# A decode-attention kernel moved from a tile framework to hand-placed buffers, semaphores and short loops

## Chip, cores and metric

One core of one Trainium2 chip; the other cores are idle. The metric is the device time of one execution in microseconds (us), a median over several runs.

Engine names: PE is TensorE (PEld its weight loads), DVE is VectorE, ACT is ScalarE, POOL is GpSimd, SP is SyncE. SP computes nothing here; it issues the loads. They are carried by 16 DMA engines.

## The reference

The function adds three terms for a batch of 8 tokens, one token each. Only the attention term is large: it reads 32 heads x 4096 keys and values of 128 numbers for each of the 8 batch entries, in bf16.

```python
xn = layernorm(A_x)                                   # (8, 1, 576)
q  = (xn @ wq) as (8, 32, 1, 128)
p  = softmax(q . k_cache * 128**-0.5)                 # k_cache (8, 32, 4096, 128)
o  = p . v_cache                                      # v_cache (8, 32, 4096, 128)
attention = o as (8, 1, 4096) @ wo                    # wo (4096, 576)
mlp = gelu(layernorm(xn) @ w1 + b1) @ w2 + b2         # w1 (576, 4608), w2 (4608, 576)
return A_x + attention + mlp
```

K and V are 2 x 268 MB; all weights together are 20 MB. There are two floating-point operations for every number read, and the profile below has the load queue at 99.5%, DVE at 65% and PE at 59%: the kernel is about moving bytes.

## The kernel before

The work is cut into 32 tiles of 8 heads. A tile's K (and its V) is 128 partitions x 64 KB = 8.4 MB. They lie in a ring of five chunks of 32 KB a partition; K and V of successive tiles take two chunks each in turn. Every fifth pair wraps around the end of the ring and is then loaded as two halves.

```python
    def chunks(t, kind):
        return [(3 + 2 * (2 * t + kind) + h) % NCH * CHUNK for h in range(2)]

    def load_kv(cache, t, at):
        src = cache_v[cache.tensor.name][bass.ds(t * P, P), :]
        if at[1] > at[0]:
            nc.sync.dma_start(out=ring[:, at[0]:at[0] + 2 * CHUNK], in_=src)
        else:
            for h in range(2):
                nc.sync.dma_start(
                    out=ring[:, at[h]:at[h] + CHUNK], in_=src[:, h * CHUNK:(h + 1) * CHUNK])
```

A tile is worked off in eight blocks: DVE multiplies a block of K with the query (`prod`), PE adds groups of the products with an identity matrix (`s_ps`), DVE reduces what is left (`sc`). ACT takes the exponential, DVE spreads it over heads (`ebd`), PE multiplies it with V (`o_ps`), and some small operations divide by the sum and store the result in `Ox`.

```python
        for x in range(2 * NCB):                       # scores of one tile
            ...                                        # DVE: prod = K block * query
            for d in range(nd):                        # PE: s_ps += identity @ part of prod
                nc.tensor.matmul(ps, lhsT=ident, rhs=prod[...], start=..., stop=...)
            if x > 0:
                reduce(x - 1)                          # DVE: sc; ACT: exp after every half
            ...
```

The main loop takes five tiles a turn, so that the ring's addresses repeat; its last turn leaves by another arm, which loads the output weights and finishes. The framework finds the waits, allots the semaphores and writes the loop's branches for all five engines.

```python
    with tc.For_i(0, LAST + NCH, NCH, iteration_sync="reg_based") as it:
        attend(it, 0)
        load_tile(it + 1, 1)
        attend(it + 1, 1)
        with tc.If(it < LAST, preferred_fallthrough_block=False) as turn:
            ...                                        # tiles 2, 3, 4 of the turn
        with turn.Else():
            project()                                  # w2, wo, last matmuls, output
```

`project()` ends with the cast of the two output halves, one on DVE and one on ACT, and their stores:

```python
        fin = const.tile([P, ND], BF16, name="fin")
        nc.vector.tensor_copy(out=fin[:B], in_=acc[0][:B])
        nc.sync.dma_start(out=out2[:, :ND], in_=fin[:B])
        nc.scalar.activation(out=fin[OP:OP + B], in_=acc[1][OP:OP + B], func=ACT.Copy)
        nc.scalar.dma_start(out=out2[:, ND:], in_=fin[OP:OP + B])
```

The softmax here doesn't subtract the row's maximum and nothing guards it: scores larger than these inputs give would overflow.

## Time and profile before

| | before |
|---|---|
| time, median | 1298.54 us (1298.42 to 1298.85, 12 runs) |
| span in the profile, first to last instruction | 1297.0 us |
| load queue: share of 16 engines, bytes, rate | 99.5%, 556.94 MB, 430 GB/s |
| busy: DVE, PE | 838.2 us (65%), 768.3 us (59%) |

These lines are from the page of the kernel before. The first gives busy time (share of the span) and instructions of each engine; "DMA" is the mean busy share, in tenths, of the 16 DMA engines in 40 equal slices of the span; "GB/s" is what they moved in each. The "q" lines are DMA queues: packets, MB, and the time of their packets as a share of 16 engines' span. q1 carries the loads, q8 and q14 carry instructions.

```profile
PE 768.3 (59%) x4780; PEld 327.0 (25%) x4780; DVE 838.2 (65%) x733; ACT 52.8 (4%) x173; POOL 1.4 (0%) x11
...
DMA  9999999999999999999999999999999999999997
GB/s 407 445 416 435 440 424 446 424 426 445 431 426 437 437 427 436 441 418 445 437 420 443 431 428 445 422 430 442 435 427 434 439 424 443 437 419 440 437 426 321
...
q1 hardware_dynamic: 12832, 556.94, 99.5%
q8 instruction: 8, 0.13, 0.0%
```

No compute engine is near its limit; the load queue is, in every slice but the last. Two more things can be read from the trace's own record of each packet (one packet is one row of a load, one partition's contiguous bytes). A row of 64 KB takes 2422 ns on its engine, a row of 32 KB 1217 ns. And from the first load packet's start (1.785 us) to the last one's end (1290.559 us) pass 1288.8 us, while all packets' time divided by 16 is 1289.0 us: the engines have no room left.

What the loads wait for, and what waits for them, is in the timeline. These are the last tile but one and the last tile of the kernel before (start, duration, engine, line, operation; in brackets the idle time before and what ended it):

```profile
1209.87 4.49 DVE L342 TENSOR_TENSOR prod<-ring,qb 128x4096 bf16<-128x4096 bf16 x2 [11.10 <-DMA ring<-in_A_k_cache_dram]
...
1222.07 0.33 SPq L142 DMA_DIRECT2D ring<-in_A_k_cache_dram  x1
...
1241.54 0.21 DVE L377 RECIPROCAL rec<-tot 128x8 f32<-128x8 f32 x1 [2.54 <-PE tot L374]
1248.44 4.50 DVE L342 TENSOR_TENSOR prod<-ring,qb 128x4096 bf16<-128x4096 bf16 x2 [4.84 <-DMA ring<-in_A_k_cache_dram]
...
1279.38 0.21 DVE L377 RECIPROCAL rec<-tot 128x8 f32<-128x8 f32 x1 [2.54 <-PE tot L374]
```

A tile's arithmetic takes some 31 us from the first product (1248.44) to the reciprocal of the sum (1279.38), when V is used up. Tiles follow each other at 38.8 us on average (that is 128 x 2 rows x 2422 ns over 16 engines). DVE waits for K between them.

The groups of instructions (busy us, mean ns of one, then idle time before them and what ended it):

```profile
L348 PE MATMUL s_ps<-prod,ident 128*128 128x512 bf16 x2048 | 564.9, 430 | 463.3 <-DVE prod L342 463.1
L342 DVE TENSOR_TENSOR prod<-ring,qb 128x4096 bf16<-128x4096 bf16 x256 | 581.9, 2284 | 176.9 <-DMA ring<-in_A_k_cache_dram 176.7
L334 DVE TENSOR_REDUCE sc<-s_ps 128x32 f32<-128x512 f32 x256 | 175.6, 686 | 98.0 <-PE s_ps L348 50.1
```

A warning about one view. The chain of waits of this kernel (work followed back from the last instruction, shares of the span) reads:

```profile
issue 40%; DMA 23%; DVE 15%; PEld 11%; PE 9%; ACT 2%; DVEq 0%; PEldq 0%; SPq 0%; ACTq 0%
```

It follows one release at a time, and goes through DVE and PE although the queue was full throughout. The packet records and the DMA row decide, not this.

### The profile page before, as it was taken

The numbers are of one execution on the slowest core, as the hardware profiler recorded it, in microseconds if no ns is written. First come the engines' busy times: TensorE is split into PE (matmuls) and PEld (weight loads), VectorE is DVE, ScalarE is ACT, GpSimd is POOL, SyncE is SP. The second block draws the span as 40 slices with busy tenths as digits, with TensorE's granted clock in tenths as the row PEclk, the third lists the DMA queues.
The fourth block names the chain that finished last, engine by engine and source line by source line (L and its number), as shares of the span: only waits on it lengthen the run. The fifth ranks groups of instructions, "written<-read, shape, count | busy, mean of one in ns | idle before, by whom it ended". The sixth has DMA issues, their size and how long they took to land.

```text
span 1297.0 us, 12687 instructions
## 1 busy us (share of the span) xinstructions
PE 768.3 (59%) x4780; PEld 327.0 (25%) x4780; DVE 838.2 (65%) x733; ACT 52.8 (4%) x173; POOL 1.4 (0%) x11
## 2 busy tenths in 40 slices
PE   5555667455666465576455566455567455567466
PEld 1122222122222222222122222122223122222123
DVE  4656677566677565677555677565677666677663
ACT  1100000000000000000000000000000000000000
POOL 0000000000000000000000000000000000000000
PEclk9788888788988778988777998787898788898779
DMA  9999999999999999999999999999999999999997
GB/s 407 445 416 435 440 424 446 424 426 445 431 426 437 437 427 436 441 418 445 437 420 443 431 428 445 422 430 442 435 427 434 439 424 443 437 419 440 437 426 321
DMA packets 12882, 557.12 MB, mean 430 GB/s; under 512 B 1452, under 2 KB 1477, under 8 KB 1735
## 3 DMA queue, kind: packets, MB, share of 16 engines
q1 hardware_dynamic: 12832, 556.94, 99.5%
q8 instruction: 8, 0.13, 0.0%
q10 hardware_dynamic: 38, 0.02, 0.0%
q14 instruction: 4, 0.02, 0.0%
HBM read 556.94 MB, written 0.01 MB: 429 GB/s over the span
## 4 chain that ended last, share of the span: by engine, by line
issue 40%; DMA 23%; DVE 15%; PEld 11%; PE 9%; ACT 2%; DVEq 0%; PEldq 0%; SPq 0%; ACTq 0%
DMA ring<-in_A_k_cache_dram 20%; PEld L348 9%; DVE prod L342 9%; PE s_ps L348 4%; PE o_ps L367 4%; DVE sc L334 3%; DVE ebd L320 3%; DMA ring<-in_A_wo_dram 2%; PEld oT L380 1%; ACT ob L371 1%; PE tot L374 1%; ACT e L314 1%; PE oT L380 1%; DMA ring<-in_A_wq_dram 0%; PEld L367 0%
## 5 line engine op out<-in xcount | busy, mean ns | idle before, releaser
L348 PE MATMUL s_ps<-prod,ident 128*128 128x512 bf16 x2048 | 564.9, 430 | 463.3 <-DVE prod L342 463.1
L342 DVE TENSOR_TENSOR prod<-ring,qb 128x4096 bf16<-128x4096 bf16 x256 | 581.9, 2284 | 176.9 <-DMA ring<-in_A_k_cache_dram 176.7
L348 PEld LDWEIGHTS <-ident 128*128 128x128 bf16 x2048 | 222.1, 108 | 798.0 <-issue 634.5
L334 DVE TENSOR_REDUCE sc<-s_ps 128x32 f32<-128x512 f32 x256 | 175.6, 686 | 98.0 <-PE s_ps L348 50.1
L367 PE MATMUL o_ps<-ring,ebd 128*32 128x512 bf16 x2048 | 122.2, 380 | 22.0 <-DVE ebd L320 22.0
L320 DVE TENSOR_TENSOR ebd<-e,head 128x1024 bf16<-128x1024 bf16 x64 | 78.1, 1221 | 16.5 <-ACT e L314 16.5
L367 PEld LDWEIGHTS <-ebd 128*32 128x32 bf16 x2048 | 48.6, 96 | 93.3 <-DVE ebd L320 37.8
L314 ACT ACTIVATE e<-sc 128x128 bf16<-128x128 f32 x64 | 19.8, 310 | 1077.6 <-DVE sc L334 1077.6
L377 DVE RECIPROCAL rec<-tot 128x8 f32<-128x8 f32 x32 | 6.6, 208 | 81.4 <-PE tot L374 81.4
L380 PE MATMUL oT<-selc,ob 128*128 128x8 f32 x256 | 33.7, 258 | 18.1 <-ACT ob L371 18.1
L380 PEld LDWEIGHTS oT<-selc,ob 128*128 128x128 f32 x256 | 31.0, 191 | 20.8 <-ACT ob L371 15.9
L382 DVE TENSOR_TENSOR on<-oT,rec 128x8 bf16<-128x8 f32 x32 | 5.3, 166 | 45.1 <-PE oT L380 43.7
L371 ACT ACTIVATE ob<-o_ps 128x512 f32<-128x512 f32 x32 | 19.1, 597 | 117.1 <-PE tot L374 117.1
L374 PEld LDWEIGHTS tot<-headf,Ep 128*128 128x128 f32 x128 | 16.6, 188 | 13.6 <-issue 13.6
L374 PE MATMUL tot<-headf,Ep 128*128 128x8 f32 x128 | 19.6, 261 | 0.0
L275 PE MATMUL h_ps<-ring,prod 128*32 128x384 bf16 x54 | 12.5, 863 | 0.0
L314 ACT ACTIVATION_READ_ACCUMULATOR e<-sc 128x1 f32 x64 | 12.0, 187 | 0.0
L286 DVE TENSOR_SCALAR prod<-prod 96x384 f32<-96x384 f32 x2 | 0.7, 352 | 13.0 <-ACT prod L285 13.0
L193 PE MATMUL tp<-ident,ring 8*128 8x8 bf16 x18 | 1.4, 198 | 12.3 <-DVE ring L189 12.3
L383 DVE TENSOR_TENSOR Ox<-on,quad 128x32 bf16 x32 | 6.2, 193 | 1.1
L308 PE MATMUL acc<-ring,OT 128*8 128x288 bf16 x64 | 4.6, 286 | 1.3 <-DMA ring<-in_A_wo_dram 1.3
L438 DVE CAST fin<-acc 8x288 bf16<-8x288 f32 x1 | 0.4, 445 | 7.3 <-PE acc L308 7.3
(67 smaller groups left out, 55.6 us busy)
## 6 DMA issues: line engine op xcount, KB each, us to landing
ring<-in_A_v_cache_dram SPq DMA_DIRECT2D x14, 4096.0 KB
ring<-in_A_k_cache_dram SPq DMA_DIRECT2D x12, 4096.0 KB, 31.7
ring<-in_B_w_dram SPq DMA_DIRECT2D x3, 1728.0 KB, 18.0
ring<-in_B_w_dram SPq DMA_DIRECT2D x2, 2592.0 KB, 30.1
ring<-in_A_wq_dram SPq DMA_DIRECT2D x3, 1536.0 KB, 9.4
ring<-in_A_wo_dram SPq DMA_DIRECT2D x1, 2016.0 KB, 24.7
ring<-in_A_wo_dram SPq DMA_DIRECT2D x1, 1440.0 KB, 25.4
ring<-in_A_wo_dram SPq DMA_DIRECT2D x1, 720.0 KB, 24.3
```

The lines of the kernel that those rows point to most:

```text
L275: nc.tensor.matmul(hps[j][s * MP:(s + 1) * MP], lhsT=lhsT, rhs=wv[:, r0:r0 + HK, :], **flags)
L314: nc.scalar.activation(out=e, in_=sc, func=ACT.Exp, scale=scale, accum_out=Ep[:, h:h + 1])
L320: nc.vector.tensor_tensor(out=ebd, in0=e[:].rearrange("p (j c) -> p j c", c=4).unsqueeze(2).to_broadcast([P, J, G, 4]), in1=head[:, :].uns ...
L334: nc.vector.tensor_reduce(out=scs[h][:, n * CB:(n + 1) * CB], in_=banks[x], axis=AX.X, op=ALU.add)
L342: nc.vector.tensor_tensor(out=prod, in0=k[h][:, n * CB:(n + 1) * CB, :], in1=qb[:, bass.ds(t, 1), :].to_broadcast([P, CB, Dh]), op=ALU.mult)
L348: nc.tensor.matmul(ps, lhsT=ident, rhs=prod[:, :, d * DL:(d + 1) * DL], start=(d == 0), stop=(d == nd - 1))
L367: nc.tensor.matmul(ps[m * MP:(m + 1) * MP, :], lhsT=ebds[h][:, j], rhs=v[h][:, 4 * j:4 * j + 4, :], start=(h == 0 and j < M), stop=(h == 1 ...
L371: nc.scalar.activation(out=ob[:].rearrange("r c d -> r (c d)"), in_=ps, func=ACT.Copy)
L374: nc.tensor.matmul(tot, lhsT=Ep[:, h:h + 1].to_broadcast([P, P]), rhs=headf, start=(h == 0), stop=(h == 1))
L377: nc.vector.reciprocal(out=rec, in_=tot)
L380: nc.tensor.matmul(oT, lhsT=ob[:, c, :], rhs=selc[:, c, :], start=(c == 0), stop=(c == 3))
L383: nc.vector.tensor_tensor(out=Ox[:, bass.ds(t, 1)].rearrange("p o g m -> p (o g) m"), in0=on[:, :].unsqueeze(2).to_broadcast([P, G, M]), i ...
```

## The change

The intent: give up the framework and its loop machinery, and place everything by hand. The arithmetic and the loaded bytes stay. What differs:

- K has two homes that overlap in one chunk, V has one home. No tile wraps, so every K and V load is one load of 64 KB rows. wq, w1 and w2 are one load each (before: 3, 3 and 2).
- One semaphore for each kind of event; the consumer waits and counts it down.
- DVE and PE loop over two tiles; ACT and SP are written out.
- The end is one wait of POOL for the output and one clearing of semaphores, without barriers.

The diff cut to its core (cuts marked):

```diff
-    def chunks(t, kind):
-        return [(3 + 2 * (2 * t + kind) + h) % NCH * CHUNK for h in range(2)]
+    def home(t, kind):
+        return 0 if kind else (3 - t % 2) * CHUNK
+
+    def load_kv(cache, t, kind):
+        at = home(t, kind)
+        nc.sync.dma_start(
+            out=ring[:, at:at + 2 * CHUNK], in_=cache[t * P:(t + 1) * P, :]
+        ).then_inc(sem["v" if kind else "k"], 16)
 ...
+    for t in range(1, NT):
+        sy.wait_ge(sem["kf"], t)          # half of K of tile t-1 used
+        load_kv(k_v, t, 0)
+        sy.wait_ge(sem["vf"], t)          # V of tile t-1 used up
+        load_kv(v_v, t, 1)
 ...
-    with tc.For_i(0, LAST + NCH, NCH, iteration_sync="reg_based") as it:
+    with nc.Fori(0, NT // 2, 1, engines=[ENG.DVE]) as it:
+        for u in range(2):
+            k = ring_k[u]
+            dtake("k", 16)
+            for x in range(2 * NCB):
+                ...
+            dtake("t")
+            ve.reciprocal(out=rec[:], in_=tot_ps[:, :G]).then_inc(sem["rf"], 1)
+            ve.wait_ge(sem["rf"], 1).then_inc(sem["vf"], 1)
+            ...
 ...
+    nc.gpsimd.wait_ge(sem["out"], 32)
+    nc.gpsimd.sem_clear(range(min(everything), max(everything) + 1))
 ...
+    with nc.Fori(0, NT // 2, 1, engines=[ENG.PE]):
+        for u in range(2):
+            tile(u)
```

The risk is plain: with a single home, V of the next tile can start to load only when V of this tile is used up. If that comes too late, the queue stands still in every tile.

## The prediction

> **What bounds the kernel now.** The DMA queue, end to end. The page's DMA view gives 99.5% of 16 engines busy on the load queue, 556.9 MB, 430 GB/s over a 1297.0 us span. In the packet records, from first to last load packet 1288.8 us pass, while the packets' own time divided by 16 engines is 1289.0 us, so there are no gaps to win. A 65536-byte row takes 2422 ns (27.06 GB/s an engine, 433 GB/s on 16), a 32768-byte row 1217 ns (431 GB/s).[...]
>
> DVE is busy 65% (838 us, 26.2 us a tile), PE 59%, neither limits. The chain of waits says "issue 40%" and "DMA 23%"; I do not trust its shares, since a tile's work, about 31 us in the timeline of the last tile (first product at 1248.4, sum ready at 1279.3), is shorter than the 38.8 us (estimate: 128 x 2 rows x 2422 ns / 16) in which its K and V arrive.
>
> **What the change does.** It replaces the tile framework with hand-placed buffers, one semaphore per event, and loops of two tiles on DVE and PE; ACT and SP are unrolled. Arithmetic and loaded bytes stay.
>
> 1. Loads: every K and V tile becomes one load of 64 KB rows. Before, 13 of 64 were cut into halves: 3328 rows of 32 KB. Estimate: (3328 x 1217 - 1664 x 2422)/16 ns = -1.2 us. wq, w1, w2 in one load each: wq's rows at 487 ns for 12 KB against 36 KB rows at the long-row rate: about -0.8 us. Together about -2 us, all critical.
> 2. V has only one home now (chunks 0-1), K two overlapping ones. V of the next tile may start only when V of this one is used up, about 31 us after K landed. The next K is in flight until about 37 to 38.8 us after that point. So the load is issued some 4 to 7 us before the queue runs dry (estimate). K's next load is released half-way through K, about 12 us in, while V is still arriving. Before, leads down to 3 us left no gap. Expect 0.
> 3. Extra wait/decrement instructions on DVE and PE: perhaps +-1 us a tile, all inside the 7 us slack: 0.
> 4. Start: wq and w1 land whole, not in thirds, so queries start some 3 us later; the first K lands at 47.3 and hides it: 0.
> 5. End: same last weight piece; the closing barriers (about 0.9 us of the span's last 1 us) are replaced by one wait and a range clear: about -0.8 us.
>
> **Predicted time: 1295.8 us**, range 1292 to 1299.5. Faster by over 2%: 1%; within 2%: 96%; slower by over 2%: 3%.
>
> **What would show it.** DMA busy 99 to 100% in nearly all slices, 431 to 432 GB/s over the span; no load packets of 32768 bytes; DVE and PE busy the same within 2%; SP waiting for PE/DVE to free V and K; DVE waiting for K some 5 to 8 us a tile as before. If step 2 is wrong, DMA share falls to 8 tenths in the slices, and the SP queue's V loads are issued after the K packets end.
>
> **What would make it wrong.** A gap of 0.8 us a tile (26 us in all) makes it slower by 2%: the single V buffer, if tile work grows from 31 to over 38 us through the added semaphore instructions. A gain of more than 6 us would need a DMA rate above 433 GB/s[...].

About -2 us for the loads and about -0.8 us for the end, from 1298.54 us, come to the 1295.8 us. What is cut is a ceiling for the DMA rate, and my exclusion of rates above 433 GB/s, which no trace or run here shows. The 433 GB/s stand as the rate of 64 KB rows in the trace (2422 ns each, on 16 engines). The "+-1 us a tile" of step 3 was a guess from no trace; the traces before and after differ by 0.6 us a tile (31.2 and 31.8 us).

## The result, and the profile after

| | before | after |
|---|---|---|
| time, median | 1298.54 us (12 runs) | 1294.53 us (1294.43 to 1294.79, 8 runs) |
| ratio | | 0.9969 (95%: 0.9959 to 0.9979) |
| span in the profile | 1297.0 us | 1292.7 us |
| first load packet starts | 1.785 us | 1.765 us |
| last load packet ends | 1290.559 us | 1289.507 us |
| last output packet ends | 1293.121 us | 1291.979 us |
| from there to the end of the span | 3.87 us | 0.68 us |

By the 2% measure it is the same; the difference of 4.0 us is nevertheless many times the spread. The lower rows come from the packet records and add up. Of the 4.33 us by which the span shrank (1296.99 to 1292.66), 0.02 us lie before the first packet, 1.03 us in the stretch of the loads, 0.09 us between the last load and the last output packet (2.56 and 2.47 us), and 3.18 us after the last byte of the output. (The output is stored in two halves by two queues; before, ACT's half landed last, 0.10 us after SP's. The expectation about the barriers below counts from SP's half and so has 3.97 and 3.29 us for 3.87 and 3.18.)

The page after, the same lines:

```profile
PE 763.9 (59%) x4780; PEld 315.8 (24%) x4780; DVE 838.2 (65%) x733; ACT 52.7 (4%) x173; POOL 1.4 (0%) x11
...
DMA  9999999999999999999999999999999999999998
GB/s 407 444 428 428 444 424 432 444 426 432 440 426 440 432 428 444 426 430 444 426 432 442 426 436 436 426 444 428 430 444 424 430 446 426 432 440 426 442 430 352
...
q1 hardware_dynamic: 10368, 556.93, 99.7%
q8 instruction: 4, 0.07, 0.0%
```

The bytes are the same, in 2464 packets less; the queue is as full as it was, and q8 fetched half as many blocks of instructions. DVE's busy time is unchanged to the tenth of a microsecond.

The timeline of the same two tiles after (L234 are the K and V loads):

```profile
1208.70 4.49 DVE L481 TENSOR_TENSOR prod<-ring,qb 128x4096 bf16<-128x4096 bf16 x2 [5.21 <-DVEq L454]
...
1221.18 0.33 SPq L234 DMA_DIRECT2D ring<-in_A_k_cache_dram  x1
...
1240.31 0.21 DVE L493 RECIPROCAL rec<-tot_ps 128x8 f32<-128x8 f32 x1 [2.75 <-DVEq L454]
1240.61 0.33 SPq L234 DMA_DIRECT2D ring<-in_A_v_cache_dram  x1
1247.40 2.29 DVE L481 TENSOR_TENSOR prod<-ring,qb 128x4096 bf16<-128x4096 bf16 x1 [5.21 <-DVEq L454]
...
1279.79 0.21 DVE L493 RECIPROCAL rec<-tot_ps 128x8 f32<-128x8 f32 x1 [2.75 <-DVEq L454]
```

Here the one home of V shows: the V load goes out at 1240.61, 0.3 us after the reciprocal that frees V. In the packet records the load before it, K, keeps the last of the 16 engines busy for another 6.1 us. Over all 31 V loads in the loop this lead is 5.3 to 6.2 us, and over the K loads 6.0 to 6.6 us. (Before, no load had a lead under 5.3 us either.)

The groups after. DVEq and PEq stand for the separate counting-down instruction that now does the waiting, so the profile no longer names what that instruction waited for:

```profile
L548 PE MATMUL s_ps<-prod,ident 128*128 128x512 bf16 x2048 | 558.9, 426 | 466.5 <-PEq L541 466.5
L481 DVE TENSOR_TENSOR prod<-ring,qb 128x4096 bf16<-128x4096 bf16 x256 | 581.9, 2284 | 156.4 <-DVEq L454 156.4
L459 DVE TENSOR_REDUCE sc<-s_ps 128x32 f32<-128x512 f32 x256 | 175.6, 686 | 109.5 <-DVEq L454 109.0
```

DVE waits 156.4 us in 32 tiles for K, 4.9 us a tile. For the same reason the chain of waits after breaks off within 20 us of the end, and is of no use:

```profile
DMA 1%; DVE 0%; SPq 0%; PE 0%; issue 0%
```

### The profile page after: what moved, and what is told of

Read it like the earlier page. It is cut to its first block, busy times and chain, and to the rows that moved or that the text cites. A ratio compares the mean times of both kernels' runs of the same rounds, so it can differ in the third digit from the quotient of the medians.

```text
span 1292.7 us, 11626 instructions
## 1 busy us (share of the span) xinstructions
PE 763.9 (59%) x4780; PEld 315.8 (24%) x4780; DVE 838.2 (65%) x733; ACT 52.7 (4%) x173; POOL 1.4 (0%) x11
## 3 DMA queue, kind: packets, MB, share of 16 engines
q1 hardware_dynamic: 10368, 556.93, 99.7%
## 5 line engine op out<-in xcount | busy, mean ns | idle before, releaser
L548 PE MATMUL s_ps<-prod,ident 128*128 128x512 bf16 x2048 | 558.9, 426 | 466.5 <-PEq L541 466.5
L481 DVE TENSOR_TENSOR prod<-ring,qb 128x4096 bf16<-128x4096 bf16 x256 | 581.9, 2284 | 156.4 <-DVEq L454 156.4
L548 PEld LDWEIGHTS s_ps<-prod,ident 128*128 128x128 bf16 x2048 | 202.9, 106 | 809.8 <-issue 664.7
L557 PEld LDWEIGHTS o_ps<-ring,ebd 128*32 128x32 bf16 x2048 | 52.2, 96 | 98.2 <-issue 58.9
L493 DVE RECIPROCAL rec<-tot_ps 128x8 f32<-128x8 f32 x32 | 6.6, 207 | 87.9 <-DVEq L454 87.9
L569 PE MATMUL oT_ps<-selc,ob 128*128 128x8 f32 x256 | 32.9, 255 | 7.9 <-PEq L541 7.9
L569 PEld LDWEIGHTS oT_ps<-selc,ob 128*128 128x128 f32 x256 | 31.0, 191 | 9.9 <-issue 9.9
L563 PEld LDWEIGHTS tot_ps<-headf,Ep 128*128 128x128 f32 x128 | 16.6, 188 | 13.6 <-issue 13.6
L563 PE MATMUL tot_ps<-headf,Ep 128*128 128x8 f32 x128 | 19.6, 261 | 0.0
L376 PE MATMUL o_ps<-ring,yT 128*32 128x384 bf16 x27 | 7.8, 861 | 2.1 <-DMA ring<-in_B_w_dram 2.1
L376 PE MATMUL x_ps<-ring,yT 128*32 128x384 bf16 x27 | 7.9, 866 | 0.0
```

What stands on the lines that cost most here:

```text
L376: i = e.matmul(h_ps[j][s * MP:(s + 1) * MP], lhsT=lhsT, rhs=wv[:, r0:r0 + HK, :], **flags)
L481: ve.tensor_tensor(out=prods[x % 2], in0=k[i][:, n * CB:(n + 1) * CB, :], in1=qb[:].rearrange("p (i u) d -> p u i d", u=2)[:, u, bass.ds(i ...
L493: ve.reciprocal(out=rec[:], in_=tot_ps[:, :G]).then_inc(sem["rf"], 1)
L548: ins = te.matmul(S_ps[x % 2].rearrange("p (c d) -> p c d", d=DL), lhsT=idn, rhs=prods[x % 2][:, :, d * DL:(d + 1) * DL], start=(d == 0), ...
L557: ins = te.matmul(o_ps[m * MP:(m + 1) * MP, :], lhsT=ebd[i][:, j].rearrange("p g c -> p (g c)"), rhs=ring_v[u][i][:, 4 * j:4 * j + 4, :], ...
L563: ins = te.matmul(tot_ps[:, :G], lhsT=Ep[:, i:i + 1].to_broadcast([P, P]), rhs=headf[:], start=(i == 0), stop=(i == 1))
```

## The experiments

There were twelve runs, one of them a repetition. "The changed kernel" took 1294.53 us, and its last load packet ended at 1289.5 us; the kernel before took 1298.3 to 1299.7 us beside these runs (medians 1298.57 to 1299.07). Three questions: where in the load stretch the 1.0 us came from, where at the end the 3.2 us came from (I had expected 2.0 and 0.8), and whether the single V buffer really costs nothing.

### Rows of 32 KB and of 16 KB

```diff
-        nc.sync.dma_start(
-            out=ring[:, at:at + 2 * CHUNK], in_=cache[t * P:(t + 1) * P, :]
-        ).then_inc(sem["v" if kind else "k"], 16)
+        w = 2 * CHUNK // PARTS                      # PARTS = 2, then 4
+        for h in range(PARTS):
+            nc.sync.dma_start(
+                out=ring[:, at + h * w:at + (h + 1) * w],
+                in_=cache[t * P:(t + 1) * P, h * w:(h + 1) * w],
+            ).then_inc(sem["v" if kind else "k"], 16)
 ...                                                # consumers wait for 16 * PARTS
```

> The changed kernel with every K and V load cut into two loads of 32 KB rows (all 64 tiles, where the kernel before cut 13), so any cost of the shorter row is multiplied by five. Theory A (row length costs DMA time, and the load queue is the bound): the packet records of the two traces give 1216.9 ns for 32 KB and 2421.8 ns for 64 KB, so 16384 x 1216.9 - 8192 x 2421.8 = 98 us of packet time, over 16 engines 6.1 us: 1300.6 us, between 1299.6 and 1301.5. Rival B (packets of neighbouring rows overlap, so the recorded duration of a packet overstates what a row costs; the 1.0 us that the last load packet came earlier is issue order, not row length): 1294.5 to 1295.5 us.

> As the run with 32 KB rows, with every K and V load cut into four loads of 16 KB rows. Theory A (each row costs a fixed few ns beside its bytes: 2 x 1216.9 - 2421.8 = 12.0 ns a cut): 24576 more rows x 12.0 ns / 16 = 18.4 us: 1312 to 1314 us. Rival B (packets overlap, nothing of it is seen): 1294.5 to 1296 us.

Measured: 1299.32 us with 32 KB rows and 1308.93 us with 16 KB rows. That is 4.79 us for 8192 more rows and 14.40 us for 24576 more rows, and both come to 9.4 ns a row and engine (4.79 us x 16 / 8192). Rival B is out. Theory A holds in kind, not in size: both times lie below its ranges. The packet records grew by 6.2 and 19.0 us, so about a quarter of what they show did not cost time. It is overlap of one packet with the next: in mid-run (60 to 1230 us) the time with more than 16 load packets under way grew by 1.4 and 4.5 us of 16 engines, nearly the whole difference. In these runs a packet's duration overstated its cost.

### The 13 cuts of the kernel before, and the weights in pieces

```diff
+        parts = 2 if (3 + 2 * (2 * t + kind)) % NCH == NCH - 1 else 1
 ...
+            ).then_inc(sem["v" if kind else "k"], 32 // parts)
```

> The changed kernel with the same 13 of its 64 K and V loads cut in halves as the kernel before cut them: 1664 more rows. The runs with all rows at 32 KB and at 16 KB cost 4.79 us for 8192 more rows and 14.40 us for 24576, both 9.4 ns a row on 16 engines. Theory A (row count alone): 1664 x 9.4 / 16 = 1.0 us more than the changed kernel, 1295.3 to 1295.7 us, and the last load packet ends 0.8 to 1.2 us later than 1289.5. Rival B (the 1.05 us by which the change moved the last load packet is fewer instruction fetches in the load queue, 3 against 7, and rows hardly count): 1294.5 to 1294.8 us.

Measured: 1295.48 us. But the kernel before, on the same chip, was at 1299.07 us (1298.67 to 1299.61) this time, and the profiled run was the slowest of the five (its last load packet ended at 1291.33 us). So I ran it again:

> The same kernel as in the run before with 13 cut loads, again, because the runs of the kernel before beside it were spread from 1298.67 to 1299.61 us and its profiled run was the slowest of its five (1296.34). Its medians left the 13 cuts at 0.4 us (against the kernel before of the same rounds) to 1.0 us (against the changed kernel's own median). Theory A (9.4 ns a row): 3.0 us below the kernel before of the same rounds (the changed kernel is 4.0 below), and the last load packet 0.8 to 1.2 us after 1289.5. Rival B (rows hardly count): 3.7 to 4.1 us below, and the last load packet before 1290.0.

Measured: 1295.37 us (1295.21 to 1295.42), and the last load packet ended at 1290.37 us, 0.86 us later than in the changed kernel and 0.19 us earlier than in the kernel before. The packet says theory A, and it leaves at most about 0.2 us to the rival, fewer instruction fetches. The difference of the medians against the kernel before of these rounds is 3.45 us, between the two theories' figures, but that kernel was spread over 1.2 us here. Taken together: the 13 cut loads cost 0.8 to 1.0 us (0.86 us by the packet, 0.95 and 0.84 us by the two medians against the changed kernel's; estimate from the row cost: 1664 x 9.4 ns / 16 = 0.98 us), which is nearly all that the load stretch gained.

```diff
-    od.load("sync", "wq", ring[:, 0:WQ_END], wq_v)
-    od.load("sync", "w1", ring[:, W1_AT:W1_END], w1_v)
+    for i in range(3):
+        od.load("sync", f"wq{i}", ring[:, ...], wq_v[:, ...])   # a third each
+    for i in range(3):
+        od.load("sync", f"w1{i}", ring[:, ...], w1_v[:, ...])
 ...                                                            # w2 in two loads
```

> The changed kernel with wq and w1 cut in three loads each and w2 in two, as before the change. My prediction took 0.8 us for these; the packet sums of the two traces say 0.03 us for wq, 0.17 us for w1, nothing for w2. Theory A (the packet sums are right, the prediction's 0.8 us was the slow first packets of the run, which come whatever is loaded first): 1294.5 to 1294.9 us. Rival B (the prediction's 0.8 us is there, hidden elsewhere): 1295.1 to 1295.5 us.

Measured: 1294.54 us, no change at all. The 12 KB rows of wq are slow in the trace of before (487 ns, 404 GB/s on 16 engines) because they are the first of the run: those of the first of the three loads take 540 ns, those of the other two 460 ns, and after the change one load of 36 KB rows at the same place runs at 405 GB/s.

### Barriers at the end

```diff
-    nc.gpsimd.wait_ge(sem["out"], 32)
-    nc.gpsimd.sem_clear(range(min(everything), max(everything) + 1))
 ...
+    sy.wait_ge(sem["out"], 32)
+    nc.all_engine_barrier()
+    nc.gpsimd.sem_clear(range(min(everything), max(everything) + 1))
+    nc.all_engine_barrier()
+    nc.all_engine_barrier()
```

> The changed kernel ended as the one before ends: SP waits for the output, then an all-engine barrier, the clearing of the semaphores, and two more all-engine barriers. The span after the last output byte shrank from 3.97 us to 0.68 us with the change, 3.29 us. Theory A (about half of this is barriers and one-by-one waits, 1.5 us from 1295.47 to 1296.95 in the trace of before; the other half is an instruction fetch on DVE after the loop's exit branch, 1292.27 to 1295.33): 1295.7 to 1296.3 us here. Rival B (the barriers are all of it): 1297.5 to 1298 us.

Measured: 1295.59 us, 1.06 us more than the changed kernel, just under theory A's range; the stretch from the last output packet to the end grew from 0.68 to 1.81 us. Putting the three barriers back restores 1.13 us, about a third of the 3.18 us. Rival B is out.

### The kernel before without its loop

```diff
-    with tc.For_i(0, LAST + NCH, NCH, iteration_sync="reg_based") as it:
-        ...
+    for t in range(NT):
+        attend(t, t)
+        if t + 1 < NT:
+            load_tile(t + 1, t + 1)
+    project()
```

> The kernel before, its loop over five tiles and its two arms written out, so that no engine takes a branch near the end; the barriers and the loads stay. Theory A (an instruction fetch behind the exit branch held DVE, and with it the closing barrier, until 1295.33, while SP, last of the others, was at the barrier at 1293.88): 1.3 to 1.8 us faster than before, 1296.7 to 1297.2 us, with DVE at its closing drain before SP. Rival B (DVE was late for another reason, or the fetch comes back at another place): 1298.2 to 1298.8 us. A time above 1299 would say that writing the loop out costs something of its own in the load queue.

Measured: 1302.44 us, 3.9 us slower. As a time this fell outside what either theory said, and only the sentence about times above 1299 fits. The trace separates two effects. The end shortened as theory A said: the stretch after the last output packet is 1.49 us instead of 3.87 us, although two of the three rounds of barriers are still in it. But the last load packet ended at 1296.57 us, 6.0 us later than before. Its DMA queues:

```profile
q1 hardware_dynamic: 12832, 556.94, 99.3%
q8 instruction: 37, 0.61, 0.2%
```

There are 37 instruction blocks of 16 KB instead of 8. In mid-run (60 to 1230 us) the time in which fewer than 16 load packets were under way comes to 2.9 us of all 16 engines, against 0.6 us before. Most of it is not idleness: an instruction block takes one engine for 0.9 to 1.1 us (in the traces before and after, 15 load packets are under way halfway through every block of the load stretch), and with the blocks counted only 0.8 us (0.2 before) are empty. The rows that were slowed beside a block (of 16 or 8 KB) took 2.8 to 3.1 us instead of the 2.42 us of a 64 KB row; another 24 rows, of 2.6 to 3.9 us, have no block beside them, and all of these started within 1 us of a moment with an engine empty. To see whether that is the fetches or something of the framework, I wrote out the loops of the changed kernel too.

```diff
-    with nc.Fori(0, NT // 2, 1, engines=[ENG.DVE]) as it:
+    for it in range(NT // 2):
 ...
-    with nc.Fori(0, NT // 2, 1, engines=[ENG.PE]):
+    for _ in range(NT // 2):
```

> The changed kernel with the loops on VectorE and TensorE written out; nothing else differs. The kernel before, written out, was 3.9 us slower instead of 1.5 us faster: its end was 2.5 us shorter, but its last load packet came 6.0 us later, with 37 instruction fetches of 16 KB instead of 8, 2.9 us of empty engine time in mid-run instead of 0.6[...]. Theory A (each fetch takes one DMA engine for about a microsecond, the engines drift apart, and those ahead run out of issued work): some 30 to 40 fetches here too, and 1297.5 to 1301 us. Rival B (what was written out of the kernel before was slow for its other loads or its waits): 1294.4 to 1295 us.

Measured: 1303.35 us (1302.78 to 1304.22), 8.8 us more than the changed kernel and more than theory A's range; the last load packet ended at 1297.82 us, 8.3 us later. Rival B is out.

```profile
q1 hardware_dynamic: 10368, 556.93, 99.3%
q8 instruction: 39, 0.64, 0.2%
```

Per additional 16 KB block the last load packet moved by 0.21 us (6.0 us for 29 blocks) and by 0.24 us (8.3 us for 35 blocks). The bytes alone would be less: 29 x 16 KB at 433 GB/s is 1.1 us (estimate). Over the whole load stretch the packet records split the 6.0 us (in time of 16 engines) into 2.1 us of carrying the blocks, 1.8 us by which the load packets themselves took longer, and 2.1 us of empty engines; the 8.3 us into 2.3, 3.2 and 2.7 us. How the last two come about is shown only in part; theory A's way, that engines ahead run out of issued work, was not shown. For the longer packets there are the rows slowed beside a block (2.8 to 3.1 us against 2.42 us, above). For the empty engines the records show one way in the changed kernel written out: five times PE itself stood for 1.1 to 2.4 us between two matmuls of one group while a block was being fetched (never in the changed kernel). V was then used up late; after three of these the V load went out late (547.6, 782.9 and 1055.5 us), and the three largest empty spells of mid-run begin within 1.4 us of these issues. The cost of a block is no constant: the load stretch holds seven blocks before the change and four after it, which at 0.2 us each would be worth 0.6 us, and the cut loads leave only 0.2 us for them.

### The kernel before, its last DVE instruction moved to ACT

```diff
-        nc.vector.tensor_copy(out=fin[:B], in_=acc[0][:B])
+        nc.scalar.activation(out=fin[:B], in_=acc[0][:B], func=ACT.Copy)
```

> The kernel before with one line changed: the last cast of the first output half goes to ScalarE, so VectorE leaves the loop after the cast of OT, some 7 us before the end, and its instruction fetch behind the exit branch lies under the wait for the last weights. Both last casts (0.40 us each) are now in a row on ScalarE, so the last output load goes out up to 0.4 us later. Theory A (that fetch held the closing barrier, from 1293.9 to 1295.4): 1297.2 to 1297.7 us, 0.8 to 1.4 us faster than before, with VectorE at its closing drain ahead of SP. Rival B (it did not, or another engine fetches as late): 1298.5 to 1299.0 us.

Measured: 1300.47 us, 1.4 us slower than before in these rounds; theory A's time was wrong, and the second half of rival B was nearer. The records of DVE and SP at the end say how. (These are the raw records of the trace: start, ns, engine, instruction; drains and semaphore waits of the closing barriers, which the page leaves out.)

```
before:
1291.65 445 DVE CAST fin          1292.21 63 DVE branch out of the loop     1293.88 7 SP drain      1295.33 135 DVE drain
instruction blocks: 16 KB at 1292.71 (0.93 us), 8 KB at 1293.57 (0.31 us)

last cast on ACT:
1285.92 63 DVE branch out of the loop     1286.04 17 DVE drain              1294.33 7 SP drain, first barrier passes
1294.73 21 DVE leaves the first barrier   1295.16 7 SP at the second        1297.52 129 DVE drain at the second
instruction block: 8 KB at 1295.76 (0.42 us)
```

Before, DVE left the loop at 1292.21 and only reached its drain, the next instruction, at 1295.33; everybody else had been at the barrier since 1293.88. With one DVE instruction fewer, the drain followed the branch at once and the first barrier passed 1.1 us earlier than before. But then DVE stood for 2.8 us between the first barrier and the second, again with an instruction block fetched in that time. So the stall did not go away; it moved by one barrier. That fits a fetch at a place in DVE's program, shifted by a few instructions, and no wait for another engine: none was late. Which engine a block was for is not recorded, so this is inferred from DVE being the only one that stood still.

In the changed kernel DVE leaves its loop some 11 us before the end (the last tile's last instruction starts at 1281.48), then waits for the last matmuls anyway, and no engine but POOL has anything to run after the output.

Together with the barriers the sum closes. From the last output packet to the end, before: 0.76 us until SP is at the barrier (1293.88), 1.59 us until DVE's drain ends (1295.47), 1.52 us for three rounds of barriers; 3.87 us in all. The same kernel written out: 0.74 us until SP's drain, then 0.74 us for two rounds without a stall; 1.49 us. So of the 2.38 us between them about 1.6 us are the stall and 0.8 us a round of barriers that went with the loop. After the change: 0.68 us (another -0.81 us).

### The single V buffer: its release held back

```diff
-            ve.wait_ge(sem["rf"], 1).then_inc(sem["vf"], 1)
+            ve.wait_ge(sem["rf"], 1).then_inc(rv, 1)
 ...
+    for t in range(NT):
+        nc.gpsimd.wait_ge(rv, t + 1)
+        for n in range(LATE):                       # LATE = 4, then 11
+            nc.gpsimd.memset(idle[:], 0.0).then_inc(ip, 1)
+            nc.gpsimd.wait_ge(ip, t * LATE + n + 1)
+        nc.gpsimd.wait_ge(rv, t + 1).then_inc(sem["vf"], 1)
```

Two earlier builds of these, with the fills not chained, were turned down by the race check before any run: two writes to one tile on POOL with nothing between them.

> The changed kernel, with the release of the V buffer held back on POOL by four chained fills of 1024 columns each (estimate 0.9 to 1.1 us each from the 0.33 us that a fill of 288 columns takes: about 4 us), DVE and PE left as they are. In the changed kernel each V load is issued 5.3 to 6.2 us before the queue would run dry, and the first packet of a load comes about 1.0 us after its issue. Theory A (a slack of 4.6 to 5 us at each V load, nothing else hangs on it): no change, 1294.3 to 1295.0 us, leads of V loads near 2 us. Rival B (the tight single V buffer already costs a little, or any delay of it does): 1296 us or more.

> The same with eleven fills, about 10 to 11 us. Theory A (slack used up; the queue then stands still between K and V. The next tile starts when its K has landed, which is two loads and about 1.7 us behind the V load of this tile, and its V release comes 32.4 us plus the delay after that; so two tile periods = 72.9 us + delay, by numbers of the trace of the changed kernel): period 41.4 to 42 us against 38.75, over 31 tiles 80 to 100 us more: 1375 to 1395 us. Theory A2 (every us beyond the slack of 4.8 us costs a whole us a tile): 31 x 5.2 to 6.2 us = 160 to 190 us more, 1455 to 1485 us. Rival B (V's single buffer is not what the queue would wait for): 1294 to 1300 us.

Measured with four fills: 1326.4 us (1323.65 to 1332.53), 31.9 us slower. Theory A's figure was wrong. The delay was as planned (timeline of that run; the V load comes 4.37 us after the reciprocal, 0.30 us in the changed kernel, so 4.07 us late):

```profile
632.15 0.21 DVE L503 RECIPROCAL rec<-tot_ps 128x8 f32<-128x8 f32 x1 [2.75 <-DVEq L456]
...
632.48 3.98 POOL L481 MEMSET idle<- 128x1024 bf16 x4 [34.69 <-DVEq L504]
...
636.52 0.33 SPq L236 DMA_DIRECT2D ring<-in_A_v_cache_dram  x1
...
640.17 4.49 DVE L491 TENSOR_TENSOR prod<-ring,qb 128x4096 bf16<-128x4096 bf16 x2 [6.14 <-DVEq L456]
```

What I had left out is that "the queue runs dry" is not one moment. Following each engine's packets from end to start, the 16 engines of the changed kernel finish the same row number about 2.1 us apart (at most 2.2), all through the run. The lead of 6.1 us is that of the last engine. The first engine has 2.1 us less, and a load's first packet comes 0.93 to 1.0 us after its issue (measured in the run with eleven fills, where the queue was empty). So the reserve is 6.1 - 2.1 - 1.0 = 3.0 us (an estimate for a V load with a long lead), and a delay of 4.07 us overdraws it by 1.07 us a tile; over 31 tiles 33 us against the 32 us measured. The match is closer than the estimate deserves. The V loads' leads to the first engine are 3.2 to 4.0 us, so the reserve is 2.2 to 3.0 us. The four runs lie 29 to 38 us above the changed kernel. And only about half of the loss in the profiled run is empty engines (17.8 of 34.1 us); the rest is load packets that took longer (16.3 us), which the sum does not have.

Measured with eleven fills: 1416.7 us (1415.5 to 1419.0), 122 us slower, with the V load 11.1 us late. Neither theory's range holds it. It is 3.94 us a tile for 11.1 us, and 2.9 us more than with four fills for 7.0 us more delay. That slope of 0.41 is near theory A's half and far from the whole of A2. Solving A's equation, two tile periods = constant + delay, gives a constant of 74.3 us from this run and 75.5 us from the other, not 72.9; the difference is about the spread of the engines, which A did not have in it. That the spread is all of the difference is not shown. Nor do the two sums fit each other: if a late release cost 0.41 us for each us from the start, the run with four fills (1.03 us a tile) would put the reserve at 4.07 - 1.03 / 0.41 = 1.6 us. So the reserve lies between 1.6 and 3.0 us (estimates), well under the lead of 6.1 us.

### Loads only

```diff
             dtake("k", 16)
-            for x in range(2 * NCB):
-                ...                                  # all of a tile's DVE work
+            for n in ("kf", "sc", "on"):             # release at once
+                ve.wait_ge(od.sem("vector"), 1).then_inc(sem[n], 1)
 ...                                                  # the same on PE for V; no ACT work
```

> A wrong result on purpose: the changed kernel without the 32 tiles' arithmetic; K and V are released as soon as they land, all else (start, weights, end) as it is. Theory A (the load queue alone sets the time from its first to its last packet, and the arithmetic neither slows a packet nor opens a gap): 1294.0 to 1294.8 us. Rival B (waiting for buffers, or DVE and PE reading the same memory, costs the queue something): below 1293 us.

Measured: 1294.44 us (1294.32 to 1294.46), with a wrong result as intended. Its page:

```profile
PE 36.9 (3%) x300; PEld 13.9 (1%) x300; DVE 17.9 (1%) x61; ACT 7.9 (1%) x13; POOL 2.6 (0%) x12
...
DMA  9999999999999999999999999999999999999998
```

Without the 32 tiles' arithmetic the kernel gains 0.09 us. The single V buffer, the semaphores, and DVE and PE reading the memory that the loads write cost nothing that can be measured. It also says that the changed kernel is at its floor for these loads, start and end: only 2.5 us lie between the last load and the last output packet. No experiment pointed to a version faster than the changed kernel, so none was tried.

## Why the prediction was right or wrong

The time was right: 1295.8 us predicted, 1294.53 us measured, inside 1292 to 1299.5. That range also held the time of the kernel before, so it was no hard test. Two terms of the sum were mis-sized in opposite directions, so the total is better than its parts, and that is luck.

- What bounds it: right. The queue is full before and after, and the loads-only kernel takes the same time as the whole one (1294.44 us).
- Step 1, loads in longer rows, "Together about -2 us": the sign is right, the size half. The last load packet came 1.05 us earlier. Its first part, -1.2 us for the 13 cut loads, measured 0.8 to 1.0 us; packet durations overstated the cost of the additional rows by about a quarter. Its second part, -0.8 us for the weights, measured 0.0 us; I had read the slow start of the run as a cost of short rows.
- Step 2, no gap from the single V buffer: right. The leads are 5.3 to 6.2 us (I said 4 to 7). But my picture of the reserve was wrong: it is at most about 3 us (estimate), because engines drift apart by 2.1 us and a load needs 1.0 us to start. "A gap of 0.8 us a tile" as what would make it slower by 2% was the right measure: a release 4.1 us later cost 1.0 us a tile, 32 us in all. The statement that tile work would have to grow "from 31 to over 38 us" for that was too generous by about 3 us: a release 4.1 us later, the same as 35 us of work, is already too late. The lead of 3 us that I read before the change, from issue times alone, was at least 5.3 us by the packets.
- Step 3, semaphore instructions: right, nothing in the time. From a tile's first product to its reciprocal pass 31.8 us on average after the change and 31.2 us before, inside the +-1 us. DVE is busy 838.2 us in both, and waits 4.9 us a tile for K after the change (5 to 8 predicted).
- Step 4, the start: right. First packets at 1.785 and 1.765 us.
- Step 5, the end, "about -0.8 us": this term failed in size. It measured -3.18 us. About 1.6 us of it are barriers and what goes with them (putting three rounds back cost 1.1 us; I had predicted 0.8). The other 1.6 us were in the trace before I predicted: DVE stood still from 1292.21 to 1295.33, beside two instruction fetches, while SP had been at the barrier since 1293.88. I looked at the last microsecond of the span, saw the barriers, and did not ask why the barrier had begun so late.

## What to carry to other kernels

Here the queue was full from end to end (99.5 and 99.7%), and the tiles' arithmetic, with its semaphores and the single V buffer, cost nothing that can be measured (1294.53 us with it, 1294.44 us without): each load was issued early enough, at least 5.3 us before the last engine ran dry. In such a kernel look first at how many rows the bytes are cut into (9.4 ns a row and engine here), and at what happens before the first and after the last byte (3.18 of the 4.33 us here). Count the lead of a load to the first engine that runs dry, not to the last (2.1 us apart here), and subtract the time that a load takes to start (0.93 to 1.0 us). Writing loops out was not free in these two kernels (3.9 and 8.8 us): an instruction block took one of the engines that carry the data for 0.9 to 1.1 us, and PE stood still for 1.1 to 2.4 us beside five of them. At the end of the kernel before one engine that stood still (DVE, 3.1 us) held the closing barrier; that was probably an instruction fetch, which is inferred.
